# Attention and a mixture of experts in one program: table limits read from PSUM, the last thresholds by another bank and queue, four tiles' weights made by VectorE

## The chip, the core and the metric

The program runs on one core of a Trainium2 chip. The metric is the time of one execution on the device, in microseconds (us), as the median of timed runs. The engines are named as the profile names them: PE (TensorE; PEld is its loading of weights), DVE (VectorE), ACT (ScalarE), POOL (GpSimd) and SP (SyncE, which here only issues DMAs). SPq and ACTq are the parts of SP and ACT that issue DMAs.

## The reference

8 batches with 8 heads each, 576 positions, head width 64. Scores below the row's maximum less tau (0.02) drop out of the softmax; the result, 4608 tokens of width 512, goes through 8 experts, one for each token.

```python
scores = scale * np.matmul(q, k.transpose(0, 1, 3, 2))
thresh = np.max(scores, axis=-1, keepdims=True) - tau
scores = np.where(scores >= thresh, scores, -1000000000.0)
attn = np.exp(scores - np.max(scores, axis=-1, keepdims=True))
attn = attn / (np.sum(attn, axis=-1, keepdims=True) + 1e-09)
x = np.matmul(attn, v)                 # then laid out as 4608 tokens x 512
logits = x @ w_gate
expert_idx = np.argmax(logits, axis=1)
gate_w = softmax(logits)[token, expert_idx]
for e in range(8):                     # tokens of expert e
    h = np.maximum(xe @ w1[e], 0.0)    # 512 -> 1024
    out[mask] = gate_w[mask, None] * (h @ w2[e])
```

## The kernel before

**Numbers in pairs.** Fp32 values are carried as two fp16 parts, hi and lo; a product is three fp16 matmuls (hi hi, hi lo, lo hi). The low part is the value less the high part; `low_part` lets PE copy the high part into a PSUM bank (tiles named hi, hi_w, hi_v) and DVE subtract from there.

**Attention** goes over 32 pairs of heads (NPAIR), 4 pairs to a batch, each in 11 steps of one tile. A pair is met twice. First `s_unit` computes the scores row by row (tile s) and DVE takes each row's maximum (nm, L370). `parts` then joins the maxima in r (L377) and `turn` makes thresholds of them: PE transposes r into a PSUM tile (pst, L381), and a chain of two ACT and two DVE steps (L386 to L389) splits the value into three fp16 rows (ptT), which `rows` copies by three DMAs into the tile CQ of the pair (L394). Second, 10 steps later, `st_unit` computes the scores transposed, less the threshold: the first matmul (L406) gives the scores, the second (L407) adds ck times CQ, and so needs the rows of ptT. ACT takes the exponent of a tile (e, L423), DVE sets to zero what lies below the threshold (the mask, L426), and two steps later `cast` rounds two tiles at once to fp16 (ph, L431, on ACT) and POOL makes the rest (pl, L432; DVE makes it for two pieces of the last pair). `av_piece` then multiplies ph and pl with v (av, L476).

The order of the tiles in the second pass is 0, 1, 2, 3, 8, 10, 9, 4, 5, 6, 7; tile 10 is the small corner, all other tiles lie in pairs in one buffer, so 4 and 5, 6 and 7.

**Routing.** When a batch is complete, `finish` divides by the sum and splits the token rows (xn, R), SP's DMAs transpose them (xTg, L545), PE forms the logits (lg, L563), and `route` and `ranks` give each token its expert and its place in a DRAM table of rows (xs), to which POOL sends it. After batches 5, 6 and 7 `counts` reads how many tokens each expert has (a PSUM bank, tile pc, and cnt on SBUF, L667), and `table_first` makes from it, in the same bank, the list of rows for the early slots of the expert stage (lim, bad, rk, has; L683 to L694). `fetch` gathers 128 rows of a slot on POOL and transposes them on SP (xTm, L859).

**Experts.** `gemm1` (h, L904) and `gemm2` (y, L937) run over slots of 128 tokens. Their first matmuls lie between the steps of the last pair, and from the end of attention on they fill PE. The weights of an expert come in 8 loads of 512 KB (wf, L793); ACT and DVE split them (wb). Those of expert 0 are split during the last pairs, with two buffers for the loads.

**Order.** The program is written step by step: `plan`, `after` and `chain` put each small piece of work at a step and into one of three slots of it. `hurry` marks what it wraps, and all that this plans later, as urgent. A scheduler then orders each engine's instructions by these priorities and by its own times for them, and from then on each engine's order is fixed. PSUM has three pools: ps_sc with 6 banks (tag sc: s, st, hi, h, half of y), ps_av with one, ps_m with one (tag m: pst, lg, rk, pc, one after the other).

In the names below, st, e, ph and pl carry the tile's number; pairs are counted from 0, so 31 is the last. `regs`, `slots` and the loop at the end for overflowing experts play no part.

## Time and profile before

| | us |
|---|---|
| median of 3 timed runs (990.03, 992.24, 993.1) | 992.24 |
| the profiled execution | 988.24 |
| its span, first to last instruction | 986.5 |
| PE busy in the span | 937.4 |
| DVE, ACT, POOL busy | 700.9, 652.9, 559.7 |
| mean granted clock of PE, of 1 | 0.992 |

Attention fills the time to about 580 us, the last batch's routing the next 40, and the expert stage the rest. Between 500 and 580 us both meet: the last pairs, the splitting of the first expert's weights, the routing of batches 5 and 6 and the first expert slots. Times in the rows are us from the span's start.

To read the rows: a row of the order of time has start, duration, engine, line, operation, output<-inputs, and in square brackets how long the engine had been idle before and what it then waited for. A granted clock of 1.00 is PE's 2.4 GHz, 0.50 its 1.2 GHz. Instructions of an engine overlap a little, so the durations of neighbours can add up to more than the time between their starts.

### The profile page before, as it was taken

Reading aid. Unit: us, or ns where it says so; the run is one execution under the profiler, and the core shown is the slowest. Engines: PE = TensorE matmul, PEld = TensorE weight load, DVE = VectorE, ACT = ScalarE, POOL = GpSimd, SP = SyncE. Lnnn points to the kernel's source line nnn. Section 1 sums busy time; section 2 is a strip of 40 time slices with the busy share of each in tenths; the row PEclk is TensorE's granted clock in tenths of the full one; section 3 lists DMA queues with packets and bytes.
Section 4 is the critical chain, followed back from the end, with each engine's and each line's share of the span. In section 5 each row is a group of like instructions: output and inputs, shape, how many; then the busy total and the mean of one; then the engine's idle time right before and its main releaser. Section 6 shows DMA issues by size and latency. Waiting matters only on the chain. (4 is left out here: it accounts for less than half of the span.)

```text
span 986.5 us, 28596 instructions
## 1 busy us (share of the span) xinstructions
PE 937.4 (95%) x11548; PEld 603.9 (61%) x11548; DVE 700.9 (71%) x1413; ACT 652.9 (66%) x1111; POOL 559.7 (57%) x467
## 2 busy tenths in 40 slices
PE   6999999999999999999997899999999999999997
PEld 2455555556566565565663576777667766667684
DVE  8899999999999999899999756817143342433560
ACT  2789897988988988989887954535243342433651
POOL 5457885996986978969958862522212121221121
PEclk9799999999999999999999999999999999999999
DMA  7643464464555646646546749999574656556630
GB/s 199 189 129 78 138 143 132 123 173 115 152 146 139 163 102 175 153 120 146 127 102 184 131 126 288 391 180 261 157 245 117 203 153 179 160 168 219 211 109 27
DMA packets 142707, 159.19 MB, mean 161 GB/s; under 512 B 96361, under 2 KB 112747, under 8 KB 142572
## 3 DMA queue, kind: packets, MB, share of 16 engines
q1 hardware_dynamic: 125782, 100.03, 40.3%
q10 hardware_dynamic: 7638, 27.85, 9.3%
q0 software_dynamic: 9152, 29.45, 9.2%
q8 instruction: 92, 1.51, 0.7%
q14 instruction: 43, 0.35, 0.1%
HBM read 90.24 MB, written 19.44 MB: 111 GB/s over the span
## 5 line engine op out<-in xcount | busy, mean ns | idle before, releaser
L432 POOL TENSOR_TENSOR pl<-e,ph 128x1024 f16<-128x1024 f32 x158 | 336.0, 2135 | 104.2 <-ACT ph L431 63.6
L423 ACT ACTIVATE e<-st,ntau 128x512 f32<-128x512 f32 (+1 forms) x352 | 222.5, 650 | 51.6 <-PE st L407 44.0
L426 DVE SCALAR_TENSOR_TENSOR e<-st,e 128x512 f32<-128x512 f32 (+1 forms) x352 | 220.2, 636 | 12.5 <-ACT e L423 11.8
L937 PE MATMUL y<-wb,hl 128*128 128x512 f16 (+1 forms) x1056 | 201.9, 360 | 0.6 <-ACT xh L491 0.6
L904 PEld LDWEIGHTS <-wb 128*128 128x128 f16 x2304 | 188.4, 98 | 21.4 <-issue 2.8
L370 DVE TENSOR_REDUCE nm<-s 128x1 f32<-128x512 f32 x300 | 188.1, 632 | 13.8 <-PE s L360 12.0
L904 PE MATMUL h<-xTm,wb 128*128 128x256 f16 (+2 forms) x2112 | 195.6, 253 | 1.4 <-issue 0.9
L476 PE MATMUL av<-vop,ph 128*128 128x65 f16 (+3 forms) x3072 | 186.8, 194 | 2.1 <-ACT x L486 2.0
L476 PEld LDWEIGHTS <-ph 128*128 128x128 f16 (+1 forms) x3072 | 157.7, 100 | 46.6 <-issue 21.7
L476 PE MATMUL av<-vop,pl 128*128 128x65 f16 (+1 forms) x1536 | 166.5, 194 | 4.1 <-POOL pl L432 4.0
L431 ACT CAST ph<-e 128x1024 f16<-128x1024 f32 x160 | 166.4, 1040 | 6.1 <-DVE e L426 5.5
L476 PEld LDWEIGHTS <-pl 128*128 128x128 f16 (+1 forms) x1536 | 136.4, 99 | 36.0 <-issue 11.4
L937 PEld LDWEIGHTS <-hl 128*128 128x128 f16 (+1 forms) x1056 | 94.1, 100 | 98.4 <-issue 2.8
L407 PE MATMUL st<-CQ,ck 128*128 128x512 f16 (+3 forms) x640 | 137.3, 289 | 3.8 <-DMA CQ<-ptT 3.8
L816 DVE SCALAR_TENSOR_TENSOR wb<-wf,wb 128x1024 f16<-128x1024 f32 x88 | 103.8, 1221 | 51.0 <-ACT wb L808 50.8
L406 PE MATMUL st<-QK 128*128 128x512 f16 (+3 forms) x640 | 138.5, 294 | 1.4 <-DVE lo L255 0.8
L358 PE MATMUL s<-QK 128*128 128x512 f16 (+1 forms) x600 | 129.3, 293 | 0.8 <-DVE e L426 0.2
L360 PE MATMUL s<-ck,CQ 128*128 128x512 f16 (+1 forms) x600 | 127.7, 288 | 0.0
L951 POOL DMA_INDIRECT out_dram<-o,gt x40 | 46.2, 1155 | 127.3 <-ACT o L948 115.9
L808 ACT ACTIVATE wb<-wf 128x1024 f16<-128x1024 f32 x96 | 97.7, 1050 | 31.2 <-DMA wf<-in_w_dram 14.7
L892 ACT ACTIVATE hl<-h 128x512 f16<-128x512 f32 (+1 forms) x80 | 45.8, 572 | 103.5 <-PE h L904 100.8
L862 DVE COPY gt<-R 128x1 f32<-128x1 f32 x33 | 5.1, 154 | 130.3 <-DMA out_dram<-o,gt 115.5
(193 smaller groups left out, 1012.1 us busy)
## 6 DMA issues: line engine op xcount, KB each, us to landing
wf<-in_w_dram SPq DMA_DIRECT2D x96, 512.0 KB
qkf<-in_qk_dram ACTq DMA_DIRECT2D x29, 576.0 KB
vf<-in_v_dram ACTq DMA_DIRECT2D x15, 640.0 KB
QK<-hi SPq DMA_DIRECT2D x62, 144.0 KB
QK<-lo SPq DMA_DIRECT2D x62, 72.0 KB
QK<-hi SPq DMA_DIRECT2D x62, 72.0 KB
ck<-lo SPq DMA_DIRECT2D x62, 72.0 KB
CQ<-hi SPq DMA_DIRECT2D x62, 64.0 KB
```

Of the source, the lines that this page charges most:

```text
L358: nc.tensor.matmul(sc[rows, oc], d["QA"][a][:, cols], d["KB"][a][:, CH[c]], start=True, stop=False)
L360: nc.tensor.matmul(sc[rows, oc], d["CQ"][:, at:at + cols.stop - cols.start], d["CK"][a][:, CH[c]], start=False, stop=True,)
L370: nc.vector.tensor_reduce(o, sc[:, 0:width(t)], axis=AX.X, op=ALU.max, negate=True)
L406: nc.tensor.matmul(sc[rows, oc], d["KB"][a][:, cols], d["QA"][a][:, CH[c]], start=True, stop=False)
L407: nc.tensor.matmul(sc[rows, oc], d["CK"][a][:, cols], d["CQ"][:, q], start=False, stop=True)
L423: nc.scalar.activation(pf, sc, AF.Exp, bias=ntau, scale=0.125 / SS)
L426: nc.vector.scalar_tensor_tensor(pf, sc, 0.0, pf, ALU.is_ge, ALU.mult)
L431: nc.scalar.copy(h, pd)
L432: (nc.vector if (n, t) in PLV else nc.gpsimd).tensor_tensor(l, pd, h, ALU.subtract)
L476: nc.tensor.matmul(av[:, 0:D] if z == 2 else av, l if z == 1 else h, vop[:, tv, W:W + D] if z == 2 else vop[:, tv, 0:W], start=i in (0, NT ...
L904: nc.tensor.matmul(o, Wt[:, c, wh, f], x, start=c == 0 and z == 0, stop=c == 3 and z == 2,)
L937: nc.tensor.matmul(o, h[:, hh], Wt[:, f, wh, c], start=f == 0 and z == 0, stop=f == 7 and z == 2)
```

## The change

Four edits:

- `table_first`: lim and has were made from cnt, which lies in SBUF (tensor_scalar with one tensor). They are now made from the counts in the PSUM bank and base_e in SBUF (scalar_tensor_tensor with two). cnt is still made, for other uses.
- `parts`, last pair only: the transposed thresholds take a bank of ps_sc, not the bank of ps_m; the turn is wrapped in `hurry`, so that its whole chain is urgent; and the three row DMAs are issued from ACT's queue, not SP's.
- `st_unit`, last pair, the last four tiles in order (4, 5, 6, 7): DVE writes ph in fp16 straight from the scores and the exponents, then masks the exponents in fp32 as before; ACT's cast is left out. pl is made as before.
- `DIRECT` names those four tiles.

```diff
@@ parts
         def turn():
-            ps = ps_m.tile([P, 512], F32, tag="m", name=f"pst_{n}")
+            pool, tag = (ps_sc, "sc") if n == NPAIR - 1 else (ps_m, "m")
+            ps = pool.tile([P, 512], F32, tag=tag, name=f"pst_{n}")
             nc.tensor.transpose(ps[0:9, 0:P], r, ident)
...
         def rows(t):
             for p in range(3):
-                (nc.sync if n >= 1 else nc.scalar).dma_start(
+                (nc.sync if 1 <= n < NPAIR - 1 else nc.scalar).dma_start(
                     st[n]["CQ"][64 + p:65 + p].rearrange("p (t c) -> p t c", t=9), t[:, p]
                 )
 
-        (after if n >= 1 else lambda k, f: hurry(f)())(1, turn)
+        if n == NPAIR - 1:
+            after(1, hurry(turn))
+        else:
+            (after if n >= 1 else lambda k, f: hurry(f)())(1, turn)
@@ st_unit
+        direct = n == NPAIR - 1 and t in DIRECT
...
         def mask():
+            if direct:
+                nc.vector.scalar_tensor_tensor(d["Ph"][t], sc, 0.0, pf, ALU.is_ge, ALU.mult)
             nc.vector.scalar_tensor_tensor(pf, sc, 0.0, pf, ALU.is_ge, ALU.mult)
...
         def cast():
-            nc.scalar.copy(h, pd)
+            if not direct:
+                nc.scalar.copy(h, pd)
             (nc.vector if (n, t) in PLV else nc.gpsimd).tensor_tensor(l, pd, h, ALU.subtract)
@@ table_first
-        nc.vector.tensor_scalar(lim[:, :, 0], cnt, -1.0, None, ALU.add)
+        nc.vector.scalar_tensor_tensor(lim[:, :, 0], bank[:, 0:E], -1.0, base_e, ALU.add, ALU.subtract)
...
-        nc.vector.tensor_scalar(has[:, :, 0], cnt, 0.5, None, ALU.is_gt)
+        nc.vector.scalar_tensor_tensor(has[:, :, 0], bank[:, 0:E], -0.5, base_e, ALU.add, ALU.is_gt)
@@ the main part
+    DIRECT = st_order[-4:]
```

The scheduler orders the program anew, so instructions move that no edit names. All is as before up to the first lim. Lines in the new kernel are some 1 to 9 higher; a name's last number is that of its buffer. Three places follow, first as the rows stood, then as they stand now.

DVE, around the first table (step of pair 30; nm are row maxima, the two L255 of wb and of vop low parts of weights and of v), before:

```order
L667 TENSOR_TENSOR cnt_12157<-pc_12155,base_e 128x8
L255 SCALAR_TENSOR_TENSOR wb_0_11668<-wf_2_0_11829,hi_w_2_0_12039 128x512
L255 SCALAR_TENSOR_TENSOR wb_0_11668<-wf_2_0_11829,hi_w_2_1_12051 128x512
L683 TENSOR_SCALAR lim_12163<-cnt_12157 128x8
L691 TENSOR_SCALAR has_12171<-cnt_12157 128x8
L370 TENSOR_REDUCE nm_11905<-s_5_12089 128x1
```

and now:

```order
L675 TENSOR_TENSOR cnt_12157<-pc_12155,base_e 128x8
L255 SCALAR_TENSOR_TENSOR wb_0_11668<-wf_2_0_11829,hi_w_2_0_12039 128x512
L255 SCALAR_TENSOR_TENSOR wb_0_11668<-wf_2_0_11829,hi_w_2_1_12051 128x512
L370 TENSOR_REDUCE nm_11905<-s_5_12089 128x1
L255 SCALAR_TENSOR_TENSOR vop_128<-vf_11717,hi_v_0_0_12093 128x5x64
L691 SCALAR_TENSOR_TENSOR lim_12163<-pc_12155,base_e 128x8
```

lim moved behind the row maximum and one low part; has, which stood right behind it, now stands 26 rows later.

ACT, around the last thresholds (ptT and CQ_126 are those of pair 31; st_2, st_3, st_8, st_10 and their e and ph are tiles of pair 30; wf_3_1 is a piece of expert 0's weights), before:

```order
L423 ACTIVATE e_2_12376<-st_2_12373,ntau 128x512
L486 COPY x_12069<-av_0_12391 128x4x65
L431 CAST ph_0_12334<-e_0_12333 128x1024
L423 ACTIVATE e_2_12376<-st_3_12407,ntau 128x512
L386 ACTIVATE ptT_12372<-pst_12370,thr 9x128
L288 ACTIVATE vop_128<-vf_11717 128x10x64
L808 ACTIVATE wb_0_11669<-wf_3_1_12216 128x2x512
L431 CAST ph_2_12377<-e_2_12376 128x1024
L388 CAST ptT_12372<-pst_12370 9x128
L423 ACTIVATE e_8_12445<-st_8_12440,ntau 128x512
```

and now:

```order
L387 ACTIVATE ptT_12372<-pst_12370,thr 9x128
L288 ACTIVATE vop_128<-vf_11717 128x10x64
L428 ACTIVATE e_2_12376<-st_2_12373,ntau 128x512
L439 CAST ph_0_12334<-e_0_12333 128x1024
L395 DMA CQ_126<-ptT_12372 1x9x128
L816 ACTIVATE wb_0_11669<-wf_3_1_12216 128x2x512
L428 ACTIVATE e_2_12376<-st_3_12407,ntau 128x512
L389 CAST ptT_12372<-pst_12370 9x128
L428 ACTIVATE e_8_12445<-st_8_12440,ntau 128x512
L395 DMA CQ_126<-ptT_12372 1x9x128
L428 ACTIVATE e_10_12476<-st_10_12471,ntau 128x64
L439 CAST ph_2_12377<-e_2_12376 128x1024
```

The chain's first step moved ahead of e_2, and the row DMAs stand among ACT's work; the third follows the last row shown.

PE, at the first scores of pair 31 (st_0 and st_1; h is the first expert slot), before:

```order
L406 LDWEIGHTS QK_0_11619
L406 MATMUL st_0_12709<-QK_0_11619 128x512
L406 LDWEIGHTS QK_0_11619
L406 MATMUL st_1_12718<-QK_0_11619 128x512
L904 LDWEIGHTS wb_0_11668
L904 MATMUL h_0_12725<-xTm_12226,wb_0_11668 128x128
```

and now:

```order
L410 LDWEIGHTS QK_0_11619
L410 MATMUL st_0_12709<-QK_0_11619 128x512
L411 LDWEIGHTS ck_0_121
L411 MATMUL st_0_12709<-CQ_126,ck_0_121 128x512
L410 LDWEIGHTS QK_0_11619
L410 MATMUL st_1_12718<-QK_0_11619 128x512
L411 LDWEIGHTS ck_0_121
L411 MATMUL st_1_12718<-CQ_126,ck_0_121 128x512
L912 LDWEIGHTS wb_0_11668
L912 MATMUL h_0_12725<-xTm_12226,wb_0_11668 128x128
```

The matmuls that need the thresholds (those with CQ_126) followed 14 matmuls of h and now stand ahead of all of them. Earlier on PE, the 48 matmuls of batch 6's logits (lg) stood together behind st_4 of pair 30; now 36 of them stand ahead of st_8, 9 ahead of hi_w_3 and st_10, 3 behind st_10. On SP, the two transposes xTg_2 that the last 24 of them read stood ahead of and behind the load wf_3_1, and now both stand behind it.

## Rows read from the trace of the kernel before

**Rows 1.** the page: busy us of each engine; PE's busy tenths in 40 slices.

```profile
PE 937.4 (95%) x11548; PEld 603.9 (61%) x11548; DVE 700.9 (71%) x1413; ACT 652.9 (66%) x1111; POOL 559.7 (57%) x467
...
PE   6999999999999999999997899999999999999997
```

**Rows 2.** stretches: us, busy of PE, PEld, DVE, ACT, POOL, granted clock, DMA.

```profile
530.00:535.00 5.00, 1.49 (x9) 0.59 (x7) 5.00 (x5) 3.04 (x8) 4.84 (x4) 1.00 0.91 232
535.00:540.00 5.00, 4.87 (x16) 1.26 (x16) 5.00 (x12) 3.16 (x4) 3.63 (x5) 0.68 0.57 147
540.00:545.00 5.00, 3.35 (x52) 2.00 (x50) 4.84 (x14) 4.37 (x7) 4.19 (x3) 0.98 0.56 182
555.00:560.00 5.00, 4.04 (x74) 2.45 (x70) 4.65 (x16) 3.36 (x8) 3.60 (x6) 1.00 1.03 130
580.00:585.00 5.00, 5.00 (x137) 4.91 (x134) 0.79 (x2) 0.50 (x2) 1.90 (x3) 1.00 0.34 104
537.00:538.00 1.00, 1.00 (x5) 0.17 (x5) 1.00 (x2) 1.00 (x3) 0.63 (x1) 0.50 0.00 0
```

**Rows 3.** order of time (start, us, what) on PE, DVE, POOL; all of L683.

```profile
534.90 0.77 PE L254 MATMUL hi_w<-wb,ident_h 128*128 128x512 f16 x2 [3.51 <-DVE nm L370]
530.37 3.81 DVE L683 TENSOR_SCALAR lim<-cnt 128x8 f32<-128x8 f32 x1
529.79 2.28 POOL L538 TENSOR_TENSOR R<-xn,R 128x512 f16<-128x512 f32 x2
532.02 2.12 POOL L432 TENSOR_TENSOR pl<-e,ph 128x1024 f16<-128x1024 f32 x1
L683 DVE TENSOR_SCALAR lim<-cnt x3: 171/172/3807, 530.4 to 613.0; 128x8 f32<-128x8 f32 x3
```

**Rows 4.** order of time, 527 to 542: POOL, loads on SP, ACT's use.

```profile
538.96 2.13 POOL L432 TENSOR_TENSOR pl<-e,ph 128x1024 f16<-128x1024 f32 x1 [1.33 <-ACT ph L431]
541.90 1.16 POOL L538 TENSOR_TENSOR R<-xn,R 128x512 f16<-128x512 f32 x1 [0.81 <-ACT R L537]
527.24 0.40 SPq L793 DMA_DIRECT2D wf<-in_w_dram  x1
530.51 0.34 SPq L793 DMA_DIRECT2D wf<-in_w_dram  x1
531.25 1.06 ACT L808 ACTIVATE wb<-wf 128x1024 f16<-128x1024 f32 x1 [0.68 <-DMA wf<-in_w_dram]
536.90 1.05 ACT L808 ACTIVATE wb<-wf 128x1024 f16<-128x1024 f32 x1
```

**Rows 5.** order of time: threshold rows of pair 31, then of the program's start.

```profile
555.71 1.55 SPq L394 DMA_DIRECT2D CQ<-ptT  x2
560.40 0.59 PE L407 MATMUL st<-CQ,ck 128*128 128x512 f16 x2 [1.36 <-DMA CQ<-ptT]
20.94 2.95 ACTq L394 DMA_DIRECT2D CQ<-ptT  x3
25.34 0.58 PE L407 MATMUL st<-CQ,ck 128*128 128x512 f16 x1 [2.27 <-DMA CQ<-ptT]
```

**Rows 6.** order of time: PE at the last logits, and transposes on SP.

```profile
595.25 0.46 PE L563 MATMUL lg<-wg,xTg 128*128 128x8 f16 x12 [1.05 <-DMA xTg<-R]
543.09 1.23 SPq L545 DMA_TRANSPOSE xTg<-R  x1
608.50 4.35 SPq L859 DMA_TRANSPOSE xTm<-Rm  x1
```

**Rows 7.** the page's groups of casts and masks; order of time on POOL, PE.

```profile
L431 ACT CAST ph<-e 128x1024 f16<-128x1024 f32 x160 | 166.4, 1040 | 6.1 <-DVE e L426 5.5
L426 DVE SCALAR_TENSOR_TENSOR e<-st,e 128x512 f32<-128x512 f32 (+1 forms) x352 | 220.2, 636 | 12.5 <-ACT e L423 11.8
577.15 2.14 POOL L432 TENSOR_TENSOR pl<-e,ph 128x1024 f16<-128x1024 f32 x1
581.37 0.19 PE L476 MATMUL av<-vop,pl 128*128 128x65 f16 x1
```

## Prediction

> **What bounds the kernel now.** I read the page's busy times first: PE is busy for 937.4 of 986.5 us, VectorE (DVE) and ScalarE (ACT) for about 700 and 650, and from the 24th slice (567 us) to the last but one PE's digit is 9, 90% or more [rows 1]. So PE sets the end, and an edit pays only where PE stands idle or runs slow. Second came the busy time by stretches of 5 us, to find those places [rows 2]: PE is busy 5.00 of 5 us in 580 to 585, but 1.49 in 530 to 535, where DVE shows 5.00; 540 to 545 and 555 to 560 leave 1.65 and 0.96 idle. With PE full behind them, I take it that what PE gains there reaches the end one for one.
>
> Third came the order of time in 530 to 535. PE stands for 3.51 us until 534.90, waiting for a row maximum of DVE, which frees a score bank [rows 3]. DVE is late because one small instruction, lim (L683, 128x8, from SBUF to SBUF), took 3.81 us from 530.37. The line runs three times; its minimum and median are 171 and 172 ns. While it hung, POOL worked without a gap: two of L538 from 529.79 to 532.07, then a pl of 2.12 us from 532.02. POOL's run ends at 534.14, lim at 534.18. I conclude that lim was held by POOL for as long as POOL worked back to back. PE's clock shows what followed: granted 0.50 in 537 to 538, its 1.2 GHz level, and 0.68 on the mean of 535 to 540.
>
> The Trainium skill, "SBUF — State Buffer", section "Who interferes with whom", says that a DVE tensor_scalar in a two-port mode and a GpSimd instruction exclude each other for the whole instruction, and that a DVE instruction with at most one SBUF input outside those modes doesn't contend. The trace agrees that lim was held, but over three POOL instructions, not one. By the one that was running (the first L538, to about 530.9) the wait would have lasted half a us, and taking it away would be worth half a us.
>
> **Part 1, limits from PSUM.** lim and has become scalar_tensor_tensor, with the counts read from PSUM and base_e from SBUF. Their number stays; lim stands two rows later in DVE's queue. The trace has no such 128x8 instruction; the masks (L426, 352 of them, mean 636 ns [rows 7]) have the same kinds of operands, and their mean lies near their own usual time although POOL works beside them most of the time. So I expect some 0.17 us, and 3.64 of the 3.81 go away.
>
> How much of that gets through? PE stood for 3.51 of it. ACT is busy 3.04 and 3.16 us in the two stretches from 530 to 540 [rows 2], so it can close up by 3.8. POOL has gaps of only 1.33 and 0.81 us up to 542 [rows 4], so it closes up by 2.1. As to weights: the load issued at 527.24 was waited for until 531.25, 4.0 us; by this measure the one issued at 530.51 could serve ACT at 534.5, not 536.90, 2.4 us earlier [rows 4]. So the ends are 2.1 us (POOL comes last) and 3.6 plus the slow clock. The clock: a mean of 0.68 over 5 us is 3.2 us at 0.50, 1.6 us of PE's work; but DVE has no idle time there and PE stood again right after, so I count none of it. I take the full 3.6, nearest to the row of DVE itself: DVE is the engine that is full there, and POOL's products are used later than they are made. **-3.6** (-2.1 to -5.2).
>
> **Part 2, last thresholds.** The transpose pst of pair 31 no longer needs the one bank of ps_m; its chain (two ACT, two DVE steps) is marked urgent, and its three row DMAs go from SP's queue to ACT's. Now SP issues the last two rows from 555.71, 1.55 us, behind transposes of the first expert slots, and PE stands 1.36 us until 560.40 for them, 3.1 us past the last issue [rows 5]. On ACT's queue, at the start of the program, three such rows were issued in 2.95 us from 20.94, and PE went on at 25.34, 1.45 us past the last issue. In the new order pst stands ahead of st_2, not behind st_3; ptT's first step stands ahead of e_2 on ACT, and the row DMAs follow ph_0, e_8 and ph_2. All three are then issued before SP's present 555.71, and PE's wait should go. Its cover goes too: 14 matmuls of h stood between the two halves of st_0, now none do, so each us of lateness is a us of PE. **-1.2** (0 to -1.4).
>
> The issues move to a nearly full ACT: 2.95 us by that row. Two of the three stand behind a cast of 1.04 us (L431 [rows 7]) that runs meanwhile, one behind an exp. If that cover failed, all 2.95 would show. SP loses three issues, which nobody waits for. **+0.3** (0 to +2.9).
>
> **Part 3, order around the logits of batch 6.** With pst gone from ps_m the scheduler pulls these ahead: 36 of the 48 lg matmuls now stand ahead of st_8, where all stood behind st_4. They need the xTg transposes, and SP now has both of the second pair behind the load wf_3_1 (one stood ahead of it). Behind lg wait st_8, hi_w_3 and st_10; behind st_10, on ACT, e_10, ph_2 and the third threshold row. For the last batch's logits PE waited up to 1.05 us for such a transpose [rows 6]; against that, PE already stands 1.65 us in 540 to 545, and a wait may only take that place. **+0.3** (0 to +1.1).
>
> **Part 4, direct weights.** For tiles 4 to 7 of pair 31 DVE writes ph itself: four instructions like L426 more, 4 x 0.64 = 2.5 us on DVE; two casts, 2 x 1.04 = 2.1 us, leave ACT [rows 7]. In DVE's new order the last e mask stands behind two hl (L893), the second of which needs h_1. PE is full there (580 to 585) with matmuls of h as filler, and DVE is busy 0.79 of those 5 us. The last pl on POOL starts at 577.15 and lasts 2.14, and PE takes a pl at 581.37 [rows 7]: 2.1 us of cover; were it used up, PE would stand for what exceeds it. **0** (-0.3 to +0.5, by the idle 0.3 us that PE has left in such a stretch and a mask's length).
>
> **Sum.** -3.6 - 1.2 + 0.3 + 0.3 + 0 = -4.2 us. The profiled execution took 988.24 us (span 986.5) and would take 984.0. The timed runs (990.03 to 993.1) all lie above it, so I subtract from their median: 992.24 - 4.2 = 988.0.
>
> **Rivals.** (A) *The hold goes, but POOL or the weight loads come last.* POOL's small gaps and the load at 530.51 speak for it, the cover of pl against it. Part 1 is then -2.1, part 3 +0.8: -2.1 - 1.2 + 0.3 + 0.8 = -2.2, 990.0.
>
> (B) *The hold isn't removed, or isn't in the timed runs.* It depends on POOL being in the middle of a run; at its other two places the line took 0.17. Part 1 is then 0, and -0.6 remains: 991.6. Against it: all queues have a fixed order, so the meeting should recur, and the new form is that of the masks.
>
> (C) *Slower: PE stands in front of the logits.* A transpose took SP 1.23 us at 543.09 but 4.35 at 608.50, beside weight loads [rows 6]. Two behind wf_3_1 at that price come 2 x 3.1 = 6.2 us later; PE has no filler, ACT's third row hangs on the same chain, and PE drops to 0.50 as before (1.6): -3.6 - 1.2 + 0.6 + 6.2 + 1.6 = +3.6, 995.8. It decides once PE's wait at lg exceeds 4.2 us. Against it: one weight load stands with them, not a row of loads.
>
> (D) *More:* the clock counts in full and A's limits don't bind; the lower ends of parts 1, 2 and 4 give -5.2 - 1.4 - 0.3 = -6.9, 985.3.
>
> **How the numbers follow.** Forecast 0.56, A 0.22, B 0.07, C 0.10, D 0.05. About 0.3% (3.0 us) is what a measurement of this kernel can tell from no change. The forecast and D are faster by more: 0.61. A and B lie within it: 0.29. C is slower: 0.10. The range goes from D less half a us, 984.8, to A without a gain from the thresholds and with half of ACT's issues in the open (-2.1 + 1.5 + 0.8 = +0.2), plus the same half us: 992.9. It leaves out C and the tails.
>
> **What would show it.** Part 1: no DVE instruction over 1.5 us in 525 to 550, PE's wait for L370 gone, granted clock 1.00 in 535 to 540. If lim still shows microseconds, B. If POOL has no idle time from 530 to 550 and PE waits for pl or hi_w instead, A. Part 2: no wait of st_0's second matmul for CQ; if there is one, the cover was worth more than I gave it. Part 3: PE's waits of lg for xTg between 540 and 555; above 4.2 us, C. Part 4: PE full from 575 to 585, av not waiting for pl. The whole is wrong if PE shows new idle time past 600, where I assume that the shift is kept.

## The result, and the profile after

The changed kernel took 998.7 us in the median of 12 runs, the kernel before 992.27 us beside it. The ratio is 1.0066, with a 95% interval from 1.0045 to 1.0087: 6.5 us slower, where 4.2 us faster was forecast, and outside the forecast's range. Timed again on three chips (the runs e9, e14 and e18 below) the same kernel stood at 0.9991, 1.0004 and 0.9999 of before. So two things have to be explained: why the gain of 4 us is nowhere to be seen, and what the first timing adds to that.

The profiled execution took 998.22 us, its span is 996.5 us. From the page, the busy times and PE's busy tenths, as [rows 1]:

```profile
PE 942.5 (95%) x11548; PEld 607.6 (61%) x11548; DVE 700.7 (70%) x1417; ACT 650.6 (65%) x1109; POOL 556.4 (56%) x467
...
PE   7999999999999999999997889899999999999997
```

PE does the same matmuls in 942.5 us in place of 937.4, so 5 of the 10 us between the two spans are matmuls that took longer (mean granted clock 0.985, before 0.992); the rest is standing. The stretches of [rows 2], and more of them (us, busy of PE, PEld, DVE, ACT, POOL, granted clock, busy share of the DMA engines, GB/s):

```profile
530.00:535.00 5.00, 3.82 (x58) 2.30 (x53) 4.45 (x13) 4.34 (x9) 4.81 (x5) 1.00 0.76 204
535.00:540.00 5.00, 3.43 (x31) 1.42 (x29) 5.00 (x11) 4.21 (x8) 4.80 (x6) 1.00 1.05 225
540.00:545.00 5.00, 2.90 (x57) 1.98 (x54) 4.27 (x11) 5.00 (x8) 5.00 (x4) 1.00 0.59 207
550.00:555.00 5.00, 3.70 (x66) 2.44 (x66) 1.32 (x3) 1.45 (x4) 3.24 (x3) 0.79 0.73 196
555.00:560.00 5.00, 5.00 (x78) 3.04 (x79) 3.98 (x14) 4.05 (x8) 3.27 (x4) 0.87 0.42 79
595.00:600.00 5.00, 1.14 (x20) 1.14 (x21) 1.80 (x3) 1.63 (x3) 1.03 (x1) 0.73 1.08 196
640.00:645.00 5.00, 3.90 (x12) 1.39 (x13) 4.32 (x15) 0.60 (x1) 2.26 (x4) 0.67 1.00 368
```

The hole in 530 to 535 is two thirds closed (3.82 us busy, before 1.49), and the clock of 535 to 540 is 1.00, before 0.68. But 535 to 545 got emptier (3.43 and 2.90, before 4.87 and 3.35), the clock falls in 550 to 560 instead, 595 to 600 holds 1.14 us of work (before 3.79), and 640 to 645 runs at 0.67 (before 1.00).

The hold itself is gone. In order of time, lim on DVE and POOL beside it (start, duration, engine, line, operation), as [rows 3]:

```profile
533.58 0.16 DVE L691 SCALAR_TENSOR_TENSOR lim<-pc,base_e 128x8 f32<-128x8 f32 x1
...
532.16 2.29 POOL L546 TENSOR_TENSOR R<-xn,R 128x512 f16<-128x512 f32 x2
534.39 2.14 POOL L440 TENSOR_TENSOR pl<-e,ph 128x1024 f16<-128x1024 f32 x1
```

All three instances of the line (minimum, median, maximum in ns, first and last start in us):

```profile
L691 DVE SCALAR_TENSOR_TENSOR lim<-pc,base_e x3: 153/161/166, 533.6 to 622.9; 128x8 f32<-128x8 f32 x3
```

lim takes 0.16 us from 533.58, in the middle of POOL's run from 532.16 to 536.5. What PE waits for now, in order of time (in brackets the idle time ahead and what ended it):

```profile
534.51 0.59 PE L254 MATMUL hi_w<-wb,ident_h 128*128 128x512 f16 x2 [0.91 <-ACT wb L816]
...
542.94 0.59 PE L254 MATMUL hi_w<-wb,ident_h 128*128 128x512 f16 x2 [2.10 <-ACT wb L816]
...
547.95 0.74 PE L571 MATMUL lg<-wg,xTg 128*128 128x8 f16 x24
551.30 0.46 PE L571 MATMUL lg<-wg,xTg 128*128 128x8 f16 x12 [2.60 <-DMA xTg<-R]
```

The same view for SP's queue, with the weight loads and the transposes of the gathered rows:

```profile
537.13 7.91 SPq L801 DMA_DIRECT2D wf<-in_w_dram  x3
545.35 2.88 SPq L553 DMA_TRANSPOSE xTg<-R  x2
```

PE gets its next hi_w at 534.51 without the 3.51 us. Then the pieces of weights come last (0.91 and 2.10 us for ACT's wb), and in the logits of batch 6, after 24 of them, PE stands 2.60 us for a transpose xTg that SP issued from 545.35, behind three weight loads. The waits of 520 to 560 in sum (us, times, longest):

```profile
PE hi_w L254 <- ACT wb L816: 5.4, 6, 2.1
PE lg L571 <- DMA xTg<-R: 2.6, 1, 2.6
```

The same for 585 to 660:

```profile
PE lg L571 <- DMA xTg<-R: 6.0, 2, 5.5
PE h L912 <- issue: 2.7, 7, 0.5
PE y L945 <- issue: 1.1, 1, 1.1
```

"issue" is a wait whose releaser the profile doesn't show. The last row of the thresholds, now on ACT's queue, as [rows 5]:

```profile
555.31 0.72 ACTq L395 DMA_DIRECT2D CQ<-ptT  x1
```

It was issued at 555.31; PE doesn't wait for CQ of pair 31 any more.

One caution in reading the two traces side by side. The first cnt, ahead of every changed row, is at 528.55 in before and at 530.77 in after. Of this, some lies at 221.8 to 225.2 us, where PE ran at 0.50 behind a wait of 0.83 us for another xTg (in before at 1.00, behind one of 0.39 us). No edit lies there, and four executions of the changed kernel reach the first cnt between 528.16 and 532.24. So the table counts from the first cnt, in us, as read from the order of time of one execution each:

| kernel | first cnt at | maxima of pair 31 joined (r) | logits of batch 6 | end of attention (last av) | first logits of batch 7 | end of the span |
|---|---|---|---|---|---|---|
| before | 528.55 | 16.3 | 25.7 to 27.1 | 55.1 | 66.7 | 458.0 |
| after | 530.77 | 13.9 | 17.2 to 24.6 | 53.5 | 68.1 | 465.7 |
| limits alone (e1) | 529.31 | 13.5 | 22.9 to 24.3 | 51.0 | 63.2 | 454.3 |
| thresholds alone (e2) | 528.59 | 16.5 | 19.9 to 23.4 | 52.6 | 65.2 | 456.1 |
| after without direct weights (e4) | 529.33 | 14.2 | 17.4 to 25.5 | 53.6 | 67.3 | 458.6 |
| limits, urgent, ACT's queue (e6) | 529.30 | 14.4 | 23.7 to 25.1 | 51.3 | 64.2 | 454.7 |
| after again (e9) | 531.92 | 14.1 | 17.4 to 24.8 | 53.6 | 66.9 | 458.4 |
| after, third time (e14) | 528.16 | 13.9 | 18.3 to 22.7 | 51.2 | 65.4 | 456.5 |
| after, second table urgent (e10) | 536.08 | 14.1 | 18.5 to 22.8 | 51.5 | 65.7 | 456.8 |

Up to r the changed kernel has gained 2.4 us on before. At the end of attention 1.6 are left, where the limits alone have 4.1. From there to the end it loses 9.3 in its first execution.

### The profile page after: what moved, and what is told of

Its sections match the earlier page's. It is cut to its first block, busy times and chain, and to the rows that moved or that the text cites. A ratio compares the mean times of both kernels' runs of the same rounds, so it can differ in the third digit from the quotient of the medians.

```text
span 996.5 us, 28592 instructions
## 1 busy us (share of the span) xinstructions
PE 942.5 (95%) x11548; PEld 607.6 (61%) x11548; DVE 700.7 (70%) x1417; ACT 650.6 (65%) x1109; POOL 556.4 (56%) x467
## 5 line engine op out<-in xcount | busy, mean ns | idle before, releaser
L433 DVE SCALAR_TENSOR_TENSOR e<-st,e 128x512 f32<-128x512 f32 (+1 forms) x352 | 220.1, 635 | 13.9 <-ACT e L428 13.2
L912 PE MATMUL h<-xTm,wb 128*128 128x256 f16 (+2 forms) x2112 | 197.8, 255 | 2.7 <-issue 2.7
L370 DVE TENSOR_REDUCE nm<-s 128x1 f32<-128x512 f32 x300 | 187.9, 632 | 14.5 <-PE s L360 12.5
L439 ACT CAST ph<-e 128x1024 f16<-128x1024 f32 x158 | 164.4, 1040 | 5.9 <-DVE e L433 5.5
L956 ACT ACTIVATE o<-y,gt 128x512 f32<-128x512 f32 (+1 forms) x40 | 26.6, 664 | 96.8 <-PE y L945 79.6
```

The lines of the kernel that those rows point to most:

```text
L370: nc.vector.tensor_reduce(o, sc[:, 0:width(t)], axis=AX.X, op=ALU.max, negate=True)
L433: nc.vector.scalar_tensor_tensor(pf, sc, 0.0, pf, ALU.is_ge, ALU.mult)
L439: nc.scalar.copy(h, pd)
L912: nc.tensor.matmul(o, Wt[:, c, wh, f], x, start=c == 0 and z == 0, stop=c == 3 and z == 2,)
```

## The experiments

The four edits are named limits, thresholds (bank, urgent, queue) and direct weights. A ratio is to the kernel before on the same chip, from 12 runs, with its 95% interval (it needn't be quite the quotient of the two medians); 0.001 is 1 us. The runs e1 to e4 shared one chip, e5 to e8 a second, e9 to e11 a third, e12 and e14 to e16 a fourth, the others a fifth.

| edits | run | ratio |
|---|---|---|
| limits | e1, e17 | 0.9966 (0.9943 to 0.9989), 0.9972 (0.9954 to 0.9990) |
| thresholds | e2 | 0.9982 (0.9960 to 1.0003) |
| direct | e3 | 0.9997 (0.9980 to 1.0014) |
| limits, direct | e7 | 0.9969 (0.9952 to 0.9986) |
| limits, urgent, queue | e6, e16 | 0.9962 (0.9939 to 0.9985), 0.9978 (0.9962 to 0.9994) |
| limits, urgent, queue, direct | e5 | 0.9987 (0.9971 to 1.0004) |
| limits, bank | e8 | 0.9995 (0.9976 to 1.0014) |
| limits, bank, direct | e11 | 1.0017 (1.0001 to 1.0033) |
| limits, thresholds | e4, e15 | 1.0009 (0.9991 to 1.0027), 0.9993 (0.9971 to 1.0015) |
| all | first result | 1.0066 (1.0045 to 1.0087) |
| all | e9, e14, e18 | 0.9991 (0.9970 to 1.0012), 1.0004 (0.9986 to 1.0022), 0.9999 (0.9984 to 1.0015) |
| all, second table urgent | e10 | 1.0014 (0.9993 to 1.0035) |

**e1, the limits alone.**

```diff
-        nc.vector.tensor_scalar(lim[:, :, 0], cnt, -1.0, None, ALU.add)
+        nc.vector.scalar_tensor_tensor(lim[:, :, 0], bank[:, 0:E], -1.0, base_e, ALU.add, ALU.subtract)
...
-        nc.vector.tensor_scalar(has[:, :, 0], cnt, 0.5, None, ALU.is_gt)
+        nc.vector.scalar_tensor_tensor(has[:, :, 0], bank[:, 0:E], -0.5, base_e, ALU.add, ALU.is_gt)
```

> The kernel before with the edit of the limits alone (lim and has from PSUM and base_e); the 48 logits of batch 6 stay together behind st_4, the thresholds and the casts as before. Theory 1 (the changed kernel lost through two new orders, that of the logits and that of the second table, while the limits did gain): no DVE instruction over 1.5 us in 525 to 550, no logits wait of PE before 560, and 1.5 to 3.6 us faster than before, since POOL and the weight loads close up by less than DVE. Theory 2 (the end of attention is sensitive to any shift: batch 7's transposes meet other transfers by chance): lim is short as well, but PE waits over 4 us for xTg in 590 to 605 and the time is within 1 us of before or above it. Theory 3 (the hold cost nothing, the weight pieces come last anyway): lim short, PE's wait for wb grows by as much, time within 0.5 us of before.

Measured: 986.22 us, 0.9966, 3.4 us faster. All instances of lim in e1:

```profile
L683 DVE SCALAR_TENSOR_TENSOR lim<-pc,base_e x3: 154/157/167, 532.0 to 624.4; 128x8 f32<-128x8 f32 x3
```

PE's waits of 520 to 560, and behind them those of 585 to 660:

```profile
PE hi_w L254 <- ACT wb L808: 4.7, 4, 2.1
...
PE st L407 <- DMA CQ<-ptT: 0.2, 1, 0.2
```

```profile
PE lg L563 <- DMA xTg<-R: 4.1, 2, 3.2
```

Theories 2 and 3 fall: the hold was worth 3.4 us by itself. Theory 2's wait of over 4 us for xTg is there (4.1), but its time isn't. The wait for wb grew from 3.8 to 4.7 us, not by what was won. And the wait for CQ of pair 31, 1.36 us before [rows 5], is 0.2 us here, though nothing was done for it. That the hold had caused it isn't shown: in three profiles with the hold and with the thresholds as before it was 0.69 us (e3), none (e12) and 0.3, the last of them in e13:

```profile
PE st L407 <- DMA CQ<-ptT: 0.3, 1, 0.3
```

The logits of batch 6 in e1, and the two transposes that the last 24 of them read:

```profile
552.20 1.36 PE L563 MATMUL lg<-wg,xTg 128*128 128x8 f16 x48
543.89 2.77 SPq L545 DMA_TRANSPOSE xTg<-R  x2
```

Here too both transposes stand behind the load wf_3_1, issued from 14.6 us past cnt as in the changed kernel. PE comes to the logits 22.9 us past cnt and doesn't wait.

**e2, the thresholds alone.**

```diff
-            ps = ps_m.tile([P, 512], F32, tag="m", name=f"pst_{n}")
+            pool, tag = (ps_sc, "sc") if n == NPAIR - 1 else (ps_m, "m")
+            ps = pool.tile([P, 512], F32, tag=tag, name=f"pst_{n}")
...
-                (nc.sync if n >= 1 else nc.scalar).dma_start(
+                (nc.sync if 1 <= n < NPAIR - 1 else nc.scalar).dma_start(
...
-        (after if n >= 1 else lambda k, f: hurry(f)())(1, turn)
+        if n == NPAIR - 1:
+            after(1, hurry(turn))
+        else:
+            (after if n >= 1 else lambda k, f: hurry(f)())(1, turn)
```

> The kernel before with the three edits of the last thresholds alone (score bank, hurry, ACT's queue). The logits of batch 6 are pulled ahead of st_8, as in the changed kernel. Theory 1: PE waits 2 to 5 us for xTg before 560, no wait for CQ of pair 31, and the time is 1 to 4 us above before. Theory 2: a wait at these logits that is made good by 580, and what is lost is lost in 590 to 605. My prediction's terms (-1.2 +0.3 +0.3) would give 0.6 us below before.

Measured: 988.1 us, 0.9982, 1.8 us faster, though the interval touches 1. All instances of lim in e2:

```profile
L687 DVE TENSOR_SCALAR lim<-cnt x3: 171/1294/3531, 530.4 to 611.5; 128x8 f32<-128x8 f32 x3
```

PE's wait for DVE in 520 to 560:

```profile
PE hi_w L254 <- DVE nm L370: 3.2, 1, 3.2
```

The first and the last group of the logits in PE's order of time:

```profile
548.50 0.62 PE L567 MATMUL lg<-wg,xTg 128*128 128x8 f16 x19
...
551.52 0.45 PE L567 MATMUL lg<-wg,xTg 128*128 128x8 f16 x12
```

The hold is back (3.53 us), and with it PE comes to the logits 19.9 us past cnt; it doesn't wait there. So the logits that are pulled ahead cost nothing as long as the hold delays PE. Both theories of a loss fall; the prediction's three terms (-0.6 us) lie within the interval.

**e3, the direct weights alone.**

```diff
...
+            if direct:
+                nc.vector.scalar_tensor_tensor(d["Ph"][t], sc, 0.0, pf, ALU.is_ge, ALU.mult)
...
-            nc.scalar.copy(h, pd)
+            if not direct:
+                nc.scalar.copy(h, pd)
...
```

> The kernel before with the direct weights alone. On DVE the second table's cnt stands behind both hl and all but one of the masks, where it stood ahead of the second hl. Theory 1: the rows of the second table are 1 to 3 us later than before (580.9), so the gathers on POOL and their transposes on SP are too, PE waits over 3 us for xTg in 590 to 605, and the time is 2 to 5 us above before. Theory 2: a loss only by chance, here as in the others. My prediction's term: 0 (-0.3 to +0.5).

Measured: 990.02 us, 0.9997. No cost, as the prediction had it; theory 1 falls.

**e4 and e15, the changed kernel without the direct weights.**

```diff
...
-            if direct:
-                nc.vector.scalar_tensor_tensor(d["Ph"][t], sc, 0.0, pf, ALU.is_ge, ALU.mult)
...
-            if not direct:
-                nc.scalar.copy(h, pd)
+            nc.scalar.copy(h, pd)
...
```

> The changed kernel without the direct weights (limits and thresholds stay). Logits and lim stand as in the changed kernel, the second table's cnt stands ahead of the second hl again. Theory 1: 2 to 5 us faster than the changed kernel, so -1 to +4 us against before, with PE's wait for xTg in 590 to 605 back to about 3 us in sum. Theory 2: that wait stays at about 6 us and the time is that of the changed kernel, 6 us above before.

> Limits and all three threshold edits without direct weights, again, now beside the changed kernel on the same chip. If direct weights cost nothing there, the two lie within 1.5 us of each other; if they cost what the first result shows, this one is 4 to 7 us lower.

Measured: 990.31 us, 1.0009; on the other chip 989.23 us, 0.9993, beside 991.16 us of the changed kernel. The time is that of e4's theory 1, the wait for batch 7's transposes isn't (4.6 us, where about 3 were expected). e15 lies 1.1 thousandths below the changed kernel, which the intervals don't separate. Limits give 3.4 us and thresholds 1.8, but both together nothing that can be told from before. PE's wait at the logits in 520 to 560, in e4:

```profile
PE lg L567 <- DMA xTg<-R: 2.7, 1, 2.7
```

What each part alone doesn't have is the wait for xTg at the logits. The limits bring PE to them 2.5 us earlier than in e2 (17.4 against 19.9 us past cnt), and the bank puts them ahead of st_8, so much earlier than in e1 (22.9).

**e5, the changed kernel with the old bank.**

```diff
-            pool, tag = (ps_sc, "sc") if n == NPAIR - 1 else (ps_m, "m")
-            ps = pool.tile([P, 512], F32, tag=tag, name=f"pst_{n}")
+            ps = ps_m.tile([P, 512], F32, tag="m", name=f"pst_{n}")
```

> The changed kernel with one thing undone: the last thresholds stay in the bank of ps_m (urgent mark, ACT's queue, limits and direct weights stay). All 48 logits of batch 6 then stand behind st_4 again, while SP still has both xTg_2 behind wf_3_1. Theory 1, now in the form that two orders cost only together (the transposes behind wf_3_1, which come with the limits, and the logits ahead of st_8, which come with the bank): no wait of PE for xTg before 560 and 2 to 5 us below before. Theory 2 (the direct weights cost what is lost, since they put the second table later): as the changed kernel, 4 to 7 us above before, with PE's wait for xTg in 590 to 605 at about 6 us.

Measured: 989.54 us, 0.9987, 1.3 us faster, though the interval touches 1: between the two theories. The wait at the logits is gone, but a new one shows. In order of time, DVE and POOL beside it:

```profile
572.23 3.54 DVE L439 TENSOR_TENSOR pl<-e,ph 128x1024 f16<-128x1024 f32 x1
...
572.54 2.14 POOL L439 TENSOR_TENSOR pl<-e,ph 128x1024 f16<-128x1024 f32 x1
```

PE's wait for it in 560 to 585:

```profile
PE av L483 <- DVE pl L439: 1.2, 1, 1.2
```

A pl on DVE (two tensors from SBUF) took 3.54 us instead of the 1.23 that it takes in before, beside a pl of POOL. In this order the two meet. PE's wait of 1.2 us is about half of what e5 lies above e6 (2.5 thousandths, which the intervals don't separate); the rest isn't explained.

**e6 and e16, limits, urgent and queue, without bank and direct weights.**

```diff
-        nc.vector.tensor_scalar(lim[:, :, 0], cnt, -1.0, None, ALU.add)
+        nc.vector.scalar_tensor_tensor(lim[:, :, 0], bank[:, 0:E], -1.0, base_e, ALU.add, ALU.subtract)
...
-                (nc.sync if n >= 1 else nc.scalar).dma_start(
+                (nc.sync if 1 <= n < NPAIR - 1 else nc.scalar).dma_start(
...
-        (after if n >= 1 else lambda k, f: hurry(f)())(1, turn)
+        if n == NPAIR - 1:
+            after(1, hurry(turn))
...
```

> Before with limits, urgent mark and ACT's queue; neither bank nor direct weights. Theory 1: no wait of PE for xTg before 560, none for CQ of pair 31, and 3 to 5 us below before (the limits alone gave 3.4). If the urgent rows on ACT's queue cost something of their own, it comes out above the run with the limits alone.

> Limits, urgent mark and ACT's queue, without bank and direct weights, again on the chip of the other two. If the bank is what takes the gain of the limits, it is 3 to 5 us below the kernel without direct weights, and 0.3 to 0.5% below before.

Measured: 986.03 us, 0.9962, and 988.18 us, 0.9978. Beside e15 on the same chip e16 is 1.5 thousandths lower, short of the 3 to 5 us expected, and the intervals don't separate the two. Over all runs the picture is clearer: with the limits and without the bank the ratios are 0.9962 to 0.9978 (e1, e6, e7, e16, e17) and 0.9987 (e5, with its wait for pl); with the limits and the bank they are 0.9991 to 1.0017 (e4, e8 to e11, e14, e15, e18) and 1.0066 (the first result). The two groups don't overlap, though e5 comes near. And urgent rows on ACT's queue add nothing to the limits that these runs can tell (0.9966 and 0.9972 without).

**e7, limits and direct weights.** The diffs of e1 and e3 together.

> Before with limits and direct weights alone. Theory 1 (direct weights cost nothing by themselves, 0.9997 of before alone): 2 to 4 us below before, as the limits alone. Theory 2 (direct weights cost once the limits have moved PE ahead, because the second table then decides when batch 7's transposes get through): 1 to 4 us above before, and the first xTg of batch 7 holds SP for over 5 us.

Measured: 986.38 us, 0.9969, as theory 1 has it. Theory 2 falls.

**e8 and e11, limits and bank, without and with direct weights.** Of the edits in `parts` only this one:

```diff
-            ps = ps_m.tile([P, 512], F32, tag="m", name=f"pst_{n}")
+            pool, tag = (ps_sc, "sc") if n == NPAIR - 1 else (ps_m, "m")
+            ps = pool.tile([P, 512], F32, tag=tag, name=f"pst_{n}")
```

> Before with limits and the score bank for the last thresholds alone; rows on SP's queue, nothing marked urgent. Logits ahead of st_8, both xTg_2 behind wf_3_1, as in the changed kernel. Theory 1: PE waits 2 to 3.5 us for xTg before 560 and the time is 0 to 3 us above before, as with limits and all three threshold edits. If that wait is not the cause of the lost 4 us, the time is 2 to 5 us below before in spite of it.

> Before with limits, bank and direct weights; thresholds neither urgent nor on ACT's queue. Limits and bank without direct weights gave 0.9995 of before. If direct weights cost only together with the urgent thresholds (in the runs so far +0.3 us on the limits, +2.5 on limits with urgent rows), it stays within 1 us of before. If they cost with the bank as well, it is 2 to 6 us above.

Measured: 989.3 us, 0.9995, and 991.71 us, 1.0017. PE's wait at the logits in 520 to 560 in e8:

```profile
PE lg L564 <- DMA xTg<-R: 2.3, 1, 2.3
```

The bank, on top of the limits, takes 2.9 thousandths back (from 0.9966 of e1) and brings the wait at the logits. e11 lies 2.2 thousandths above e8, on another chip, between the two forms expected; its wait at the logits is 2.6 us. What direct weights cost with the bank stays open.

**e9, e14 and e18, the changed kernel again.** No edit.

> The changed kernel once more, timed beside the other parts. If the loss past the logits belongs to the kernel, it comes out 4 to 8 us above before, and its profile shows PE standing without a visible releaser between 105 and 115 us past the first cnt, as in its first profile (637 to 643). If that stand was one of this execution, it is missing here, and the time lies near that of limits and thresholds without direct weights (0.9 above before) or up to 3 us above.

> The changed kernel a third time (0.66% above before on the first chip, 0.09% below on the second), beside the same without direct weights and the same without bank and direct weights. If the first difference belonged to that chip and hour, it comes out within 0.3% of before, 3 to 4 us above the kernel with limits and urgent rows alone; if it belongs to the kernel on most chips, 0.4 to 0.8% above before.

> The changed kernel a fourth time, beside the limits alone. If the 0.66% of the first chip belongs to that chip, it comes out within 0.3% of before, as on two other chips (0.9991 and 1.0004); if such chips are common, again 0.5% or more above.

Measured: 990.56, 991.16 and 990.84 us; 0.9991, 1.0004 and 0.9999. So the 0.66% didn't recur. PE's wait at batch 6's logits in e9:

```profile
PE lg L571 <- DMA xTg<-R: 2.5, 1, 2.5
```

And in e18:

```profile
PE lg L571 <- DMA xTg<-R: 2.6, 1, 2.6
```

It is there in both; a stand without releaser past 605 is in neither. The profiled execution of e14 was one of its quick ones (986.46 us, where the median of its 12 is 991.16). Its logits in PE's order of time:

```profile
546.42 1.27 PE L571 MATMUL lg<-wg,xTg 128*128 128x8 f16 x36
...
549.69 0.38 PE L571 MATMUL lg<-wg,xTg 128*128 128x8 f16 x9 [0.25 <-DMA xTg<-R]
```

The transposes on SP's queue:

```profile
542.75 3.32 SPq L553 DMA_TRANSPOSE xTg<-R  x2
```

They were issued 14.6 us past cnt, as in the first profile of the kernel (545.35 is 14.6 past its 530.77). But there the 25th logit, the first to read them, was let go at 551.30, 5.95 us behind the issue, and in e14 36 of them ran through by 547.69, 4.9 us behind it, without a wait; PE also came 1.1 us later (18.3 past cnt, not 17.2). The nine after them waited 0.25 us. Its attention ended 51.2 us past cnt, as with the limits alone. So the wait is a race of PE with the landing of the transposes, and the landing isn't the same in each execution; why, no run shows.

**e10, the second table urgent.**

```diff
-                after(wait + dist * n, TABLES[b])
+                after(wait + dist * n, hurry(TABLES[b]) if b == B - 2 else TABLES[b])
```

> The changed kernel with the second table marked urgent: its cnt stands ahead of the eight masks of tiles 4 to 7 on DVE, not behind them; PE's order and SP's are those of the changed kernel. If the late second table is what the direct weights cost (gathers and their transposes later, batch 7's transposes behind them), rows of the second table come 2 us or more earlier and the time falls by 3 to 6 us against the changed kernel, to that without direct weights. If it isn't, the time stays within 1.5 us of the changed kernel.

Measured: 992.01 us, 1.0014. In e10 the second cnt stands 38.5 us past the first (47.9 in e9) and its rows come 3.2 us earlier, but the time doesn't fall. So the place that the direct weights leave the second table wasn't what cost. PE's wait at batch 6's logits, in 520 to 560:

```profile
PE lg L571 <- DMA xTg<-R: 0.3, 1, 0.3
```

As in e14, PE hardly waits there, and attention ends 51.5 us past cnt. The execution as a whole was the longest of its 12 (994.66 us), but its first cnt, at 536.08, came 4 to 8 us later than in the four profiles of the changed kernel, and no edit lies ahead of it.

**e12 and e13, what is held.** Two probes on the kernel before. In e12 lim becomes another operation, but all its tensors stay in SBUF; in e13 lim reads PSUM, moves back in the order, and has takes its place.

```diff
-        nc.vector.tensor_scalar(lim[:, :, 0], cnt, -1.0, None, ALU.add)
+        nc.vector.scalar_tensor_tensor(lim[:, :, 0], cnt, -1.0, cnt, ALU.add, ALU.min)
```

```diff
-        nc.vector.tensor_scalar(lim[:, :, 0], cnt, -1.0, None, ALU.add)
+        nc.vector.tensor_tensor(bank[:, 8:8 + E], bank[:, 0:E], base_e, ALU.subtract)
+        nc.vector.tensor_scalar(lim[:, :, 0], bank[:, 8:8 + E], -1.0, None, ALU.add)
```

> A probe on the kernel before: lim as scalar_tensor_tensor, both tensors the cnt in SBUF ((cnt - 1) min cnt), at its old place right behind the low parts of wb. If what holds lim is a second SBUF operand or a form of two ports, whatever the operation, its first instance takes 3 to 4 us as before. If it is the form tensor_scalar alone, 0.17 us.

> A probe on the kernel before: lim stays tensor_scalar, but reads a copy of the counts in PSUM; has stays tensor_scalar from SBUF and now stands where lim stood, right behind the low parts of wb. If the hold belongs to the place and to an instruction whose tensors all lie in SBUF, has now takes 3 to 4 us at its first instance and lim 0.17. If it belonged to lim or to the name cnt alone, neither does.

Measured. All instances of lim in e12:

```profile
L683 DVE SCALAR_TENSOR_TENSOR lim<-cnt x3: 166/261/3271, 531.1 to 615.1; 128x8 f32<-128x8 f32 x3
```

POOL beside the first of them, in order of time:

```profile
529.96 2.29 POOL L538 TENSOR_TENSOR R<-xn,R 128x512 f16<-128x512 f32 x2
532.20 2.13 POOL L432 TENSOR_TENSOR pl<-e,ph 128x1024 f16<-128x1024 f32 x1
```

All instances of has and of lim in e13:

```profile
L692 DVE TENSOR_SCALAR has<-cnt x3: 216/712/3379, 532.8 to 620.5; 128x8 f32<-128x8 f32 x3
...
L684 DVE TENSOR_SCALAR lim<-pc x3: 153/166/166, 538.7 to 632.0; 128x8 f32<-128x8 f32 x3
```

The hold stays with scalar_tensor_tensor (3.27 us from 531.1, so until 534.4, and POOL's run ends at 534.33) and moves to has (3.38 us from 532.77, and POOL's run ends at 536.11). The first lim of e13, tensor_scalar from PSUM, took 0.15 us at 538.72, while POOL worked. The hold belongs to the place and to operands that all lie in SBUF, not to the operation.

**e17, the limits alone again**, with the diff of e1, beside e18.

> The limits alone, again, beside the changed kernel on one chip: 2 to 4 us below before and 2 to 5 us below the changed kernel, if the other edits give back what the limits gain; equal to the changed kernel otherwise.

Measured: 986.9 us, 0.9972, beside 990.84 us, 0.9999, of the changed kernel. The limits alone beat both kernels: 2.8 thousandths below before, 2.7 below the changed kernel.

## Why the prediction was wrong

**What bounds the kernel: right for the limits.** PE sets the end. With the limits alone the gain, by the table, is 2.8 us at r, 4.1 at the end of attention, 3.5 at batch 7's first logits (PE, being earlier, waits 4.1 us there in place of 2.4) and 3.7 at the end: it is kept. The changed kernel doesn't keep it: in e9 1.5 us are left at the end of attention and none at batch 7's first logits, where PE waits 4.2 us. So "one for one" holds only as far as that wait doesn't take up what was won.

**Part 1: right in mechanism and about in size.** -3.6 us was forecast, -3.4 and -2.8 were measured. lim took 3.3 to 3.8 us in every profile that had it at that place with all operands in SBUF, 0.15 to 0.17 in every one with the new operands. POOL or the weight loads didn't come last by much (rival A): the wait for wb grew by 0.9 us in e1 and 1.2 in e17. The Trainium skill, "SBUF — State Buffer", section "Who interferes with whom", says that a DVE instruction with at most one SBUF input, outside the two-port modes, doesn't contend with GpSimd, and that one with two contends with a GpSimd instruction that reads SBUF. The runs agree: the new lim has one (0.15 to 0.17 us), e12's has two (3.27 us). The old lim and e13's has are tensor_scalar with one SBUF input and were held as well; whether they ran in a two-port mode no trace shows. The hold also lasted longer than one GpSimd instruction, to the end of POOL's run of three.

**Part 2: right by itself, wrong in the sum.** -1.2 was forecast, -1.8 measured alone. On top of the limits (e6 and e16 against e1 and e17; without the bank) it is between -1.0 and +1.2 thousandths, whichever are paired, because the wait for CQ is already 0.2 us there. Two terms read from one trace were added, though the second wait didn't hold in other profiles: with the thresholds as before it was 1.36, 0.69, 0.3 us or none beside the hold, and 0.2 without it. ACT's issues, +0.3, can't be seen.

**Part 3: the step that failed.** "+0.3 (0 to +1.1)" for the order around the logits should have been about +3. The groups with and without the bank differ by 3 us (0.9991 to 1.0017 against 0.9962 to 0.9978, the first result and e5 left out). PE's wait for xTg at batch 6's logits is 2.3 to 2.7 us in seven of the nine profiles with limits and bank, and there attention ends 53.5 to 54.4 us past cnt. It is 0.25 and 0.3 in the other two (e14 and e10), and there attention ends at 51.2 and 51.5, as without the bank (50.9 to 51.9 in e1, e6, e7, e16 and e17; 53.1 in e5, with its wait for pl). The prediction weighed how much later SP would issue the transposes. They aren't issued later: from 545.35, that is 14.6 us past cnt, and in before at 543.09 and 546.31, 14.5 and 17.8 past it. What moved is PE. In before its logits and the second transpose stood like this:

```profile
554.28 1.36 PE L563 MATMUL lg<-wg,xTg 128*128 128x8 f16 x48
546.31 1.23 SPq L545 DMA_TRANSPOSE xTg<-R  x1
```

So PE came to the logits 25.7 us past cnt, and now it comes at 17.2, 8.5 us earlier. By that difference the transposes had some 6 us of slack in before (an estimate: 8.5 less the wait of 2.6), and it is used up. The sentence that "a wait may only take that place" of PE's idle time was the wrong choice between the ends. Rival C had the mechanism (PE stands ahead of the logits) and a chance of 0.10; it asked for more than 4.2 us of wait to end slower, and by the three repeats the wait of 2.6 us ends at no change. SP's order, with both transposes behind the load, isn't enough for the wait: e1 has it and doesn't wait. Whether it is needed wasn't separated: e2, which doesn't wait either, has both a later PE and the old order of one transpose ahead of the last load. And no run has the bank with the logits kept behind st_4.

The granted clock doesn't tell the kernels apart. It is 1.00 in 535 to 540, as forecast, but 0.79 and 0.87 in 550 to 560. In e1, which has neither the hold nor the stand at the logits, it is 0.68 in 540 to 545. So the fall only moved, and leaving it out of part 1 was right.

**Part 4: right on before and on the limits, open beside the threshold edits.** 0 was forecast; -0.3 and +0.3 thousandths were measured on before (e3) and on the limits (e7 against e1). It was +1.1 on limits and thresholds (e14 against e15), +2.2 on limits and bank (e11 against e8) and +2.5 without the bank (e5 against e6), there in part by a meeting of two pl that no term held. None of these is clear of the intervals, but the range of +0.5 looks too narrow.

**What is left open.** Between the forecast (-4.2 us) and the first result (+6.5) lie 10.7 us. Parts 2 and 3, as the repeats show them, account for about 4 of these, which makes no change out of the gain. The other 6 to 7 were met in the first timing only, where the changed kernel lies 0.66% above before; in the three repeats it lies within 0.1% of it. In the first profile 7.3 us more than in e9 lie between the first cnt and the end, 6 of them past batch 7's first logits: PE stood 3.8 us in 8 pieces with no releaser shown (most of it in 637 to 643), and the clock fell to 0.67 in 640 to 645. The wait for batch 7's xTg was 6.0 us in place of e9's 4.2. In the three later profiles PE is busy without a gap from 635 to 655 and its granted clock there is 1.00. The prediction's last condition, new idle time of PE past 600, is met in this one of the four profiles of the kernel. Whether that is the chip, or a meeting of transfers that this kernel is more prone to, the runs don't tell.

## What to carry to other kernels

Don't add up waits from one trace: one may be smaller in the next execution or once another is removed, and an engine that arrives earlier may find new ones. Ask of each transfer that is hidden now how much slack hides it, and take from that slack what the other edits win and what the order gives away; here PE came to the logits 8.5 us earlier by two edits, neither of which alone made it wait there. And try the edits one by one: one edit of the four, the limits, gave all of the gain that lasted.

## What the runs showed of the hardware

- A DVE instruction whose tensors all lie in SBUF was held until POOL's run of three instructions ended: 3.81, 3.53, 3.41, 3.27 and 3.38 us, in two operations, against 0.15 to 0.17 with PSUM as a source. A larger one, pl, took 3.54 us beside a single POOL instruction of 2.14 (e5), and 2.22 and 2.71 beside POOL's work in the changed kernel and in e1; in before it takes 1.23.
- Two transposes on SP, issued behind weight loads, let PE go on 5.95 us after the issue in the first profile of the changed kernel (5.9 to 6.3 in all seven executions with limits and bank that wait), and in less than 4.9 in another (e14), with SP's issues ahead of them at the same distance from cnt to within 0.3 us.
- PE ran at 0.50, its 1.2 GHz level, from 221.8 to 225.2 us behind a stand of 0.83 us, and before did not behind one of 0.39. The length of the stand doesn't decide it: in e1, behind one of 0.84 us at the same place, the clock stayed at 1.00. Four executions of the changed kernel differ by up to 4.1 us ahead of any changed row (the first cnt), in part by such a fall, so stretches are better compared from a common event than from the start.
